# FC2 of a two-layer block as Strassen products over a finished FC1, with streamed weight sums

## The chip, the core and the metric

The kernel runs on one core of a Trainium2 chip. A core has a matrix engine (TensorE, PE in the profile), a vector engine (VectorE, DVE), a scalar engine (ScalarE, ACT), a general engine (GpSimd, POOL) and a sync engine (SP) that issues DMAs; 16 DMA engines move data between device memory and the on-chip memory SBUF. TensorE writes its sums to PSUM, which has eight banks of 512 float32 columns. The metric is the device time of one execution in microseconds, the median of several runs; lower is better.

## What is computed

Two layers, each an attention block and a feed-forward block (FFN) with a residual, over 2048 tokens of 640 channels:

```python
def _A_ref(x, wqkv, wo):                       # 32 heads of 20
    qkv = (x @ wqkv).reshape(B, S, 3, H, Dh).transpose(2, 0, 3, 1, 4)
    q, k, v = qkv[0], qkv[1], qkv[2]
    phi = lambda t: jnp.where(t > 0, t + 1, jnp.exp(t)) + 1e-6
    pq, pk = phi(q), phi(k)
    kv = jnp.einsum("bhsd,bhse->bhde", pk, v)
    z = jnp.einsum("bhsd->bhd", pk)
    num = jnp.einsum("bhqd,bhde->bhqe", pq, kv)
    den = jnp.einsum("bhqd,bhd->bhq", pq, z)[..., None] + 1e-6
    return (num / den).transpose(0, 2, 1, 3).reshape(B, S, D) @ wo

def _B_ref(x, w1, b1, w2, b2):                 # 640 -> 1728 -> 640
    r = jnp.maximum(jnp.einsum("bsd,df->bsf", x, w1) + b1, 0)
    return jnp.einsum("bsf,fd->bsd", r * r, w2) + b2

for _ in range(2):
    x = x + _A_ref(_layernorm(x, axis=-1), A_wqkv, A_wo)
    x = x + _B_ref(_layernorm(x, axis=-1), B_w1, B_b1, B_w2, B_b2)
```

## The kernel before

Every large product is made of three matmuls in the type float32r, as `mm3` does: each operand is split into a high half (a copy rounded to float32r, made by ScalarE) and a low half (the rest, a subtraction on VectorE), and high x low, low x high and high x high are added in PSUM. The tokens are 16 tiles of 128, or 4 groups (`NG`) of 4 tiles (`TG`).

A layer has three parts.

*The first stage* walks over the 16 tiles. Each is normed (`ln_stats`, `ln_apply`), turned so that the channels stand on the partitions, split, and multiplied with the q and k columns of wqkv (`part`). `Phi` applies the feature map. `g_part` and `gt_part` add the products of k features and x into G and GT, from which the small matrix M is made that stands for all of attention behind the q features. Turning a tile is VectorE's transpose of 32x32 blocks (`blocks_T`) followed by 16 copies on ScalarE that put the blocks in place (`blocks_move`); the first tiles of a layer are turned by TensorE (`transpose5`). The q part of the tiles in `LATE` is computed after the loop (`late_q`). In layer 0 this stage also prepares the FFN's weights (`Prep`): it loads a unit, splits it, and keeps it in device memory as `kept_w`. A unit is 128 rows of w2, or 128 columns of w1, with both halves, 640 KB. `PREP` says how many are done at each tile.

*The turn to the FFN* builds M and carries the first four tiles through the attention output, their residual, norm and turn.

*The FFN* runs group by group, and in a group chunk by chunk over the 1728 hidden channels (`NF` = 14 chunks, the last of 64). `fc1` computes a chunk for the 512 tokens of the group, 15 matmuls of 512 columns; `act` applies bias, relu and square and splits the result (one ScalarE and three VectorE operations of 128x512); `fc2` of the chunk before adds its part to the five outputs of the group (the 512 first columns of the four tiles, and the 128 last columns of all four as one turned "strip"), 5 x 3 matmuls of 512 columns. So FC1 and FC2 alternate every 3.4 us. At the end of a group the strip is turned back (`strip_turn`), and the sums are added to x1, which had been kept in device memory (`f_bias` stores it with the bias b2, `x1_load` loads it). The units of chunks 4 and 7 stay in SBUF (`RESIDENT`); the others come through a ring of six buffers (`load_ring`), 24 units a group.

Between the matmuls of a group stands the side work for the next one: the denominators of attention (`b_ops`), the turn and split of the q features, the attention output, residual, norm, turn and split of x. `single` does it tile by tile (group 1 of a layer), with 30 matmuls of 320 columns a tile; `side` with `Pair` does it for two tiles at once with seven Strassen products of 54 matmuls (groups 2 and 3), whose mixed operands are made by `m_turns` and `s_turns`. Where each step stands is written by hand: `events` maps a group, a chunk and a place to the steps. Each engine works strictly in the order in which its instructions are written, SP's queue of DMAs too, and waits at the head of its queue for whatever its next instruction needs. The last group of layer 0 prepares the first tiles of layer 1 in the same way (`side_last`).

## Time and profile before

| | |
|---|---|
| median of 3 runs | 1351.71 us (1351.32 to 1351.85) |
| span of the profiled execution | 1349.9 us |
| TensorE clock granted | 1.000 |
| layer 0: first stage and turn / four FFN groups | 0 to 255 us / 255 to 679 us |
| layer 1: first stage and turn / four FFN groups | 679 to 922 us / 922 to 1346 us |
| DMA traffic | 253.44 MB, mean 188 GB/s |

The page gives for each engine the time in which it executes something; matmuls overlap, so a row's mean duration (389 ns for 512 columns) is not the spacing at which they follow one another. Rows of groups read: line, engine, operation, out<-in, shape, count, busy us, mean ns of one, idle us before them and what ended it. Rows of the timeline read: start us, length us, engine, line, operation, out<-in, shape, count. Rows of the windows read: stretch, its length, then busy us and number of instructions of PE, PEld (weight loads), DVE, ACT and POOL, the granted clock, the busy share of the DMA engines and GB/s. A row of DMA issues gives KB each and the us from issue to landing.

### The profile page before, as it was taken

The numbers are of one execution on the slowest core, as the hardware profiler recorded it, in microseconds if no ns is written. First come the engines' busy times: TensorE is split into PE (matmuls) and PEld (weight loads), VectorE is DVE, ScalarE is ACT, GpSimd is POOL, SyncE is SP. The second block draws the span as 40 slices with busy tenths as digits, with TensorE's granted clock in tenths as the row PEclk, the third lists the DMA queues.
The fourth block names the chain that finished last, engine by engine and source line by source line (L and its number), as shares of the span: only waits on it lengthen the run. The fifth ranks groups of instructions, "written<-read, shape, count | busy, mean of one in ns | idle before, by whom it ended". The sixth has DMA issues, their size and how long they took to land.

```text
span 1349.9 us, 18967 instructions
## 1 busy us (share of the span) xinstructions
PE 1342.1 (99%) x6797; PEld 1158.3 (86%) x6797; DVE 911.7 (68%) x1627; ACT 770.3 (57%) x1932; POOL 123.4 (9%) x174
## 2 busy tenths in 40 slices
PE   9999999999999999999999999999999999999998
PEld 8888998888888888888888899988888888888887
DVE  7888757777777676643467676677778667775323
ACT  5878858676546448411447688494756446464110
POOL 2222210000000000000012232100000000000000
PEclk9999999999999999999999999999999999999999
DMA  6787835574665475387521115156546646644734
GB/s 205 254 301 269 284 86 177 192 275 145 212 237 174 158 292 170 117 327 293 184 98 51 48 40 155 41 206 255 173 157 232 216 150 223 233 167 140 287 125 158
DMA packets 85635, 253.44 MB, mean 188 GB/s; under 512 B 11030, under 2 KB 19606, under 8 KB 84902
## 3 DMA queue, kind: packets, MB, share of 16 engines
q1 hardware_dynamic: 85398, 252.04, 53.7%
q8 instruction: 54, 0.88, 0.3%
q14 instruction: 39, 0.32, 0.1%
q10 hardware_dynamic: 144, 0.20, 0.0%
HBM read 193.50 MB, written 56.03 MB: 185 GB/s over the span
## 4 chain that ended last, share of the span: by engine, by line
PE 92%; DVE 3%; ACT 3%; DMA 1%; issue 1%; POOL 0%; SPq 0%; DVEq 0%; ACTq 0%
PE PS L395 34%; PE PS L1064 28%; PE PS L1114 28%; ACT z L381 2%; PE PS L911 1%; PE PS L924 1%; DMA st<-in_A_wqkv_dram 1%; PE PS L726 0%; DVE bn L352 0%; DVE xr L658 0%; DVE e L498 0%; DVE xTb L131 0%; DMA Mr<-Mc 0%; DVE r L499 0%; PE PS L1128 0%
## 5 line engine op out<-in xcount | busy, mean ns | idle before, releaser
L381 ACT ACTIVATE z<-y 32x160 f32<-32x160 f32 x1424 | 475.8, 334 | 75.2 <-DVE y L372 59.0
L1064 PE MATMUL PS<-xTb,u 128*128 128x512 f32 x1400 | 333.8, 390 | 1.0 <-DVE xTb L131 1.0
L1064 PEld LDWEIGHTS PS<-xTb,u 128*128 128x128 f32 x1400 | 261.6, 188 | 55.0 <-DVE xTb L131 1.5
L395 PE MATMUL PS<-kq,xT 128*128 128x320 f32 (+2 forms) x1575 | 284.4, 334 | 0.4 <-DVE GT L529 0.4
L1114 PE MATMUL PS<-u,h 128*128 128x512 f32 x1120 | 276.8, 390 | 0.0
L395 PEld LDWEIGHTS PS<-kq,xT 128*128 128x128 f32 x1575 | 250.1, 188 | 28.2 <-DVE rl L499 1.0
L1114 PEld LDWEIGHTS PS<-u,h 128*128 128x128 f32 x1120 | 208.5, 188 | 40.8
L1076 ACT ACTIVATE hr<-PS,b1sb 128x512 f32<-128x512 f32 x104 | 71.4, 687 | 297.6 <-PE PS L1064 296.9
L1077 DVE TENSOR_TENSOR hr<-hr 128x512 f32<-128x512 f32 x104 | 71.8, 690 | 217.4 <-ACT hr L1076 216.9
L395 PE MATMUL PS<-kh,xh 128*128 128x512 f32 x480 | 124.6, 393 | 0.0
L491 ACT ACTIVATE e<-PS 128x320 f32<-128x320 f32 (+4 forms) x128 | 53.5, 435 | 101.9 <-PE PS L395 93.5
L356 POOL TENSOR_SCALAR rs<-mv 128x1 f32<-128x1 f32 x64 | 28.0, 438 | 869.6 <-DVE mv L354 869.6
L395 PE MATMUL PS<-uM,pT 128*128 128x320 f32 x648 | 102.6, 309 | 0.7 <-DVE uM L940 0.7
L395 PEld LDWEIGHTS PS<-kh,xh 128*128 128x128 f32 x480 | 87.2, 188 | 15.6 <-DVE kh L690 0.4
L395 PEld LDWEIGHTS PS<-uM,pT 128*128 128x128 f32 x648 | 97.7, 188 | 3.1 <-DVE uM L940 1.2
L498 DVE TENSOR_SCALAR e<-e 128x320 f32<-128x320 f32 (+4 forms) x128 | 41.7, 325 | 80.0 <-ACT e L491 79.7
L1114 PE MATMUL PS<-h,u 128*128 128x512 f32 x280 | 79.0, 390 | 0.0
L1079 DVE TENSOR_TENSOR h<-hr,h 128x512 fp32r<-128x512 f32 x104 | 72.0, 693 | 3.6
L687 POOL TENSOR_TENSOR acc<-acc,r 128x640 f32<-128x640 f32 x30 | 53.8, 1795 | 198.5 <-DVE r L499 198.5
L1114 PEld LDWEIGHTS PS<-h,u 128*128 128x128 f32 x280 | 52.2, 188 | 10.8 <-DVE h L1090 0.4
L1064 PE MATMUL PS<-xTb,uw 128*128 128x512 f32 x240 | 57.0, 389 | 0.0
L499 DVE SCALAR_TENSOR_TENSOR r<-PS,e 128x512 f32<-128x512 f32 (+2 forms) x104 | 51.1, 492 | 5.8 <-ACT e L491 2.4
(126 smaller groups left out, 1353.9 us busy)
## 6 DMA issues: line engine op xcount, KB each, us to landing
u<-kept_w SPq DMA_DIRECT2D x184, 640.0 KB, 4.3
x<-x SPq DMA_DIRECT2D x48, 320.0 KB, 6.3
kept_w<-uprep SPq DMA_DIRECT2D x23, 640.0 KB, 4.9
pqt<-pq SPq DMA_DIRECT2D x32, 320.0 KB, 5.6
x<-xr SPq DMA_DIRECT2D x32, 320.0 KB, 2.4
st<-in_B_w_dram SPq DMA_DIRECT2D x22, 320.0 KB, 5.6
pq<-r SPq DMA_DIRECT2D x20, 320.0 KB
kept_kq<-kq SPq DMA_DIRECT2D x10, 640.0 KB, 5.7
```

Source lines behind the costliest of these rows:

```text
L356: nc.gpsimd.tensor_scalar(rs, mv[:, 1:2], LN_EPS, None, op0=ALU.add)
L381: nc.scalar.activation(zv[j * B32 : (j + 1) * B32, :, i, :], yv[i * B32 : (i + 1) * B32, :, j, :], AF.Copy)
L395: nc.tensor.matmul(ps, a, b, start=first and i == 0, stop=last and i == 2)
L491: nc.scalar.activation(self.e[:, a:b], ps, AF.Exp)
L498: nc.vector.tensor_scalar(e, e, 1.0, PHI_EPS, op0=ALU.min, op1=ALU.add)
L499: nc.vector.scalar_tensor_tensor(out=self.r[:, a:b], in0=ps, scalar=0.0, in1=e, op0=ALU.max, op1=ALU.add)
L687: nc.gpsimd.tensor_tensor(out=acc, in0=acc, in1=r, op=ALU.add)
L1064: nc.tensor.matmul(ps, a[:, d, :], bb[:, d, :], start=d == 0 and i == 0, stop=d == DC - 1 and i == len(seq) - 1,)
L1076: nc.scalar.activation(r, ps, AF.Relu, bias=b1sb[:, c : c + 1])
L1077: nc.vector.tensor_tensor(out=r, in0=r, in1=r, op=ALU.mult)
L1079: nc.vector.tensor_tensor(out=h[:, 1], in0=r, in1=h[:, 0].bitcast(F32), op=ALU.subtract)
L1114: nc.tensor.matmul(ps, l, r, start=first and k == 0, stop=last and k == len(a) - 1)
```

## The change

FC2 becomes Winograd's form of Strassen's product: the 512 tokens of a group are two halves of 256, the hidden channels two halves of 7 x 128 (padded with zeros from 1728 to 1792), the 640 outputs two halves of 320. Seven products replace eight. For that, the group's FC1 is finished first and its squared result R stays in SBUF in float32. Then FC2 runs in 28 steps: the products in `ORDER`, each in four units of two row blocks (the last of one).

- `act` no longer splits; it writes R. `s_op` forms the four sums of quarters of R in place (VectorE), `u_hi` (ScalarE) and `u_lo` (VectorE) split the operand of a step into one of five slots (`arena`), four steps ahead.
- `fc2_step` is, for each row block and each of the two token tiles, three matmuls of 320 columns. The products of one output are chained in one PSUM bank (`CHAIN`), and `fc2_add` adds the state of the chain to x1 after a product, straight in SBUF; x1 is no longer stored and loaded again. There are no strips.
- The four sums of w2's quarters are formed in layer 0's first stage: `Prep` takes w1 units ("a") and pairs of w2 rows ("t"), for which GpSimd makes four sums (`mix`); one step of it stands at four places of each tile (`prep_step`). In the FFN one unit in four of each product stays in SBUF, the other three and all of w1 come through the ring.
- The attention output of all tiles is done singly; `side`, `Pair`, `m_turns` and `s_turns` are gone.
- x is turned in another order of channels (channel 5p + c in place of 128c + p; the rows of wqkv and w1 are loaded to match). In layer 1's first stage and in the FFN a tile is stored by GpSimd's DMA queue and loaded by four DMAs with 32 rows in runs of 160 elements (`spread_out`, `spread_in`); VectorE's transpose (`turn`) then finishes it, with no copies on ScalarE. In layer 0's first stage and the first two tiles of each FFN the 16 copies stay (`turn_move`).
- The bias b2 is added by GpSimd (`f_bias`). The pool of general tiles has 8 buffers in place of 12, and a new pool of 4 holds x1 and raw weights. The kq blocks are kept at tiles 11 to 15 instead of 6 to 15.

```diff
-RESIDENT = (4, 7)
 RING = 6
+KH = 7
+PAIRS = 4
+ORDER = (1, 5, 6, 2, 7, 3, 4)
+N_STEPS = len(ORDER) * PAIRS
+SLOTS = 5
+HT = GT // 2
...
-PREP = {t: 2 if t > 5 else 3 for t in range(2, 12)}
+PREP = {2: "aaa", 3: "t", 4: "t", 5: "aaaa", 6: "t", 7: "t", 8: "aaaa", 9: "t", 10: "t", 11: "aaa", 12: "t"}
+PREP_AT = range(1, 14)
...
-F_BUFS = 12
+F_BUFS, X_BUFS = 8, 4
+OUTS = (4, 7, 10, 13)
...
+        def mix(self):
...
+            def sub(out, x, y, op=ALU.subtract):
+                nc.gpsimd.tensor_tensor(out=out, in0=x, in1=y, op=op)
+
+            sub(q[:, lo], a[:, hi], a[:, lo])
+            sub(q[:, hi], b[:, hi], a[:, hi])
+            sub(a[:, hi], q[:, hi], a[:, lo], ALU.add)
+            self.raws.append(((p, (2, 3)), b, 2 * D))
+            self.raws.append(((p, (5, 7)), q, 2 * D))
+            self.raws.append(((p, (1, 6)), a, 2 * D))
...
+    def spread_out(src):
...
+        nc.gpsimd.dma_start(d, src)
+        return d
+
+    def spread_in(d):
+        z = ftile("z")
+        for j in range(JQ):
+            nc.sync.dma_start(
+                z[j * B32 : (j + 1) * B32].rearrange("p (i f) -> p i f", f=Q),
+                d[:, j * Q : (j + 1) * Q].rearrange("(i q) f -> q i f", q=B32),
+            )
+        return z
+
+    def turn(z):
+
+        y = ftile("y")
+        nc.vector.transpose(
+            out=y.rearrange("p (c i q) -> p i c q", c=DC, q=B32),
+            in_=z.rearrange("p (i q c) -> p i c q", c=DC, q=B32),
+        )
+        return y
...
+        def prep_step(t, i):
+            if layer == 0 and t in PREP_AT:
+                if i == 0:
+                    prep.mix()
+                prep.low()
+                prep.high()
+                if i == 3:
+                    prep.load(PREP.get(t + 1, ""))
...
         def f_bias(t):
 
-            v = xr.pop(t)
-            nc.vector.tensor_tensor(out=v, in0=v, in1=b2bc, op=ALU.add)
-            nc.sync.dma_start(x1d[t], v)
+            v = xr[t]
+            nc.gpsimd.tensor_tensor(out=v, in0=v, in1=b2bc, op=ALU.add)
...
+        def comb(out, x, y, k, op):
+            nc.vector.tensor_tensor(out=quad(*out, k), in0=quad(*x, k), in1=quad(*y, k), op=op)
...
+        def u_hi(g, n):
+            v, u = unit(g, n)
+            nc.scalar.activation(u[:, 0], v, AF.Copy)
+
+        def u_lo(g, n):
+            v, u = unit(g, n)
+            nc.vector.tensor_tensor(out=u[:, 1], in0=v, in1=u[:, 0].bitcast(F32), op=ALU.subtract)
...
+        def fc2_step(g, n, i, first, last):
...
+            for p in range(b - a):
+                h, l = (u[:, j, p, i * P : (i + 1) * P] for j in range(2))
+                for e, (x, y) in enumerate(((h, w[:, 1, p]), (l, w[:, 0, p]), (h, w[:, 0, p]))):
+                    nc.tensor.matmul(
+                        ps, x, y, start=opens and k == 0 and p == 0 and e == 0,
+                        stop=k == PAIRS - 1 and p == b - a - 1 and e == 2, skip_group_check=True,
+                    )
...
+        def single(g, i):
...
+            n = NF + (1, 5, 9, 13)[i]
+            at(g, n, load)
+            steps(lambda: x_split(t), (g, n + 4), (g, n + 5), (g, n + 6))
+
+        def ffn_events(g):
...
+            for n in range(PAIRS + 1, N_STEPS):
+                at(g, s + n - 4, lambda n=n: u_hi(g, n))
+                at(g, s + n - 4, lambda n=n: u_lo(g, n))
...
+            at(g, 2, lambda: load_kq(0))
+            for c, n in ((1, 5), (2, 13), (3, 21), (4, 25)):
+                at(g, s + n, lambda c=c: load_kq(c))
...
         for g in range(NG):
             for c in range(NF):
                 ps = fc1(g, c)
                 wu.load_ring()
+                act(c, ps)
+                run(g, ("pe", c))
+                run(g, c)
...
+            for n in range(last if tail else N_STEPS):
+                for i in range(2):
+                    fc2_step(g, n, i, False, False)
+                wu.used(g, ORDER[n // PAIRS], n % PAIRS)
+                wu.load_ring()
+                run(g, NF + n)
```

829 lines of the change are left out of this document (315 added, 514 removed).

## The prediction

> **What bounds the kernel now.** I read the page first, then the PE rows by form, then the timeline for the spacing of matmuls.
>
> ```profile
> span 1349.9 us, 18967 instructions
> PE 1342.1 (99%) x6797; PEld 1158.3 (86%) x6797; DVE 911.7 (68%) x1627; ACT 770.3 (57%) x1932; POOL 123.4 (9%) x174
> ...
> PEclk9999999999999999999999999999999999999999
> ...
> PE 92%; DVE 3%; ACT 3%; DMA 1%; issue 1%; POOL 0%; SPq 0%; DVEq 0%; ACTq 0%
> ```
>
> TensorE is busy in 1342.1 of 1349.9 us at an undisturbed clock, and 92% of the chain that ended last is matmuls. Only 7.8 us are left between them. So the time can fall only if TensorE gets less work, and it rises as soon as another engine makes it wait. The forecast is a count of matmuls, plus the waits that the new side work may cause.
>
> A busy PE is not yet a price, since matmuls overlap. The price is the distance between starts:
>
> ```profile
> 240.06 4.56 PE L395 MATMUL PS<-uM,pT 128*128 128x320 f32 x30
> 244.46 4.57 PE L395 MATMUL PS<-kq,xT 128*128 128x320 f32 x30
> ...
> 265.44 3.56 PE L1064 MATMUL PS<-xTb,u 128*128 128x512 f32 x15
> 268.84 2.88 PE L1114 MATMUL PS<-u,h 128*128 128x512 f32 x12
> ...
> 1342.02 0.60 PE L1128 MATMUL PS<-ident,strip 128*128 128x128 f32 x4
> 1342.38 3.69 PE L1114 MATMUL PS<-u,h 128*128 128x512 f32 x15
> ```
>
> 30 matmuls of 320 columns take 244.46 - 240.06 = 4.40 us, so 146.7 ns each; 15 of 512 columns take 3.40 us, so 226.7 ns each. That is 0.417 ns a column and a fixed 13.4 ns. The four strip transposes take 0.36 us.
>
> **The change on TensorE.** The counts, by form (FC2 is L1114, the attention output is what reads pT or uS):
>
> ```profile
> L1114 PE MATMUL PS<-u,h 128*128 128x512 f32 x1120 | 276.8, 390 | 0.0
> L1114 PE MATMUL PS<-h,u 128*128 128x512 f32 x280 | 79.0, 390 | 0.0
> L1114 PE MATMUL PS<-uw,h 128*128 128x512 f32 x192 | 46.1, 389 | 0.0
> L1114 PE MATMUL PS<-h,uw 128*128 128x512 f32 x48 | 13.5, 389 | 0.0
> ...
> L395 PE MATMUL PS<-uM,pT 128*128 128x320 f32 x648 | 102.6, 309 | 0.7 <-DVE uM L940 0.7
> L395 PE MATMUL PS<-uT,uS 128*128 128x320 f32 x144 | 25.0, 309 | 0.0
> L395 PE MATMUL PS<-uM,uS 128*128 128x320 f32 x72 | 11.8, 308 | 0.0
> L395 PE MATMUL PS<-uT,pT 128*128 128x320 f32 x48 | 8.3, 309 | 0.0
> ```
>
> FC2 before: 1640 matmuls in 8 groups, 205 each (13 chunks of 3 passes and one of 2, by 5 outputs), so 205 x 226.7 = 46.5 us a group. After: 7 products x 7 row blocks x 2 token tiles x 3 passes = 294 of 320 columns, so 294 x 146.7 = 43.1 us. The gain is 3.34 us a group, **26.7 us** in all: a tenth fewer columns, of which the 89 extra fixed costs take a quarter back. The 32 strip transposes go: 8 x 0.36 = **2.9 us**. The attention output was 912 matmuls and becomes 32 tiles x 2 halves x 5 x 3 = 960: 48 x 146.7 = **7.0 us** lost. FC1 and the first stage keep their matmuls. Net: -26.7 - 2.9 + 7.0 = **-22.6 us**.
>
> On the Trainium skill's page "TensorE: Matmul & The Clock Gate", section "Back-to-back issue gap", a sustained stream of weight load and matmul is given as about 81 ns at 128 columns and 131 ns at 512. By a line through these (an estimate) 320 columns would cost 106 ns, and FC2 would go from 205 x 131 = 26.9 to 294 x 106 = 31.2 us a group, 35 us lost in all. The rows above differ from both figures, so the measurement decides.
>
> **The side work in the FFN.** FC2 now stands in one block of 28 steps (1.76 us a step, 0.88 every fourth), and what VectorE does there was spread over FC1 before. Its spacings:
>
> ```profile
> 486.55 0.69 DVE L1079 TENSOR_TENSOR h<-hr,h 128x512 fp32r<-128x512 f32 x1
> 487.16 0.55 DVE L1284 TENSOR_TENSOR pT<-z,pT 128x384 fp32r<-128x384 f32 x1
> 487.74 2.01 DVE L1267 TENSOR_TENSOR z<-z 128x256 f32<-128x256 f32 x5
> ...
> 498.36 0.49 DVE L1335 TENSOR_TENSOR su<-PS,uu 128x320 f32<-128x320 f32 x1 [0.66 <-PE PS L395]
> 498.76 0.48 DVE L1335 TENSOR_TENSOR xr<-PS,xr 128x320 f32<-128x320 f32 x1
> 499.16 0.88 DVE L352 BATCH_NORM_STATS2 bn<-xr 128x6 f32<-128x320 f32 x2
> ...
> 505.34 0.85 DVE L372 STREAM_TRANSPOSE y<-xn 128x640 f32<-128x640 f32 x1
> 506.11 0.78 DVE L1335 TENSOR_TENSOR xr<-su,xr 128x640 f32<-128x640 f32 x1
> ```
>
> From start to start 512 columns cost 0.61 us, 256 cost 0.40, a PSUM addition of 320 costs 0.40, a transpose 0.77. One FC2 block holds 23 low halves (17 x 0.61 + 6 x 0.40 = 12.8), 13 sums of R (9 x 0.61 + 4 x 0.40 = 7.1), 12 additions (4.8), four turns and low halves of x (4 x 1.5 = 6.0), the last tile's addition and norm (0.8 + 0.9 + about 0.8) and the next tile's denominator and scaling (about 3.5 from the same widths): 36.7 us of 43.1. The low half of a unit is asked for 4 steps (6.2 us) before TensorE needs it, so VectorE may lag by some 4.9 us (6.2 less the high half on ScalarE, about 0.65, and the low half itself) before a matmul waits. It fits, with little to spare. The bias addition moves to POOL, and that is not free:
>
> ```profile
> 118.63 1.62 POOL L687 TENSOR_TENSOR acc<-acc,r 128x640 f32<-128x640 f32 x1 [7.09 <-DVE r L499]
> 119.33 1.61 DVE L131 TENSOR_TENSOR xh<-xt,xh 128x640 fp32r<-128x640 f32 x1
> 129.66 0.82 DVE L131 TENSOR_TENSOR xh<-xt,xh 128x640 fp32r<-128x640 f32 x1
> ```
>
> Beside a POOL operation of 1.62 us the same VectorE subtraction takes 1.61 instead of 0.82 us. One such bias falls into FC2: 0.8 us more, 37.5 in all (87%). I book **+2 us** for the six groups that carry side work. The lower bound is 0 (the lag absorbs all); the upper is the slower rival below. ScalarE loses the 16 block moves of each x tile (5.5 us, the row at 130.43 below), and its high halves fit.
>
> The weights: without the pairing, FC2 streams 3 of 4 units of each product. Including the next FC1's six, that is 18.5 full units of 640 KB, and ten transfers of 320 KB: 15.4 MB in 43.1 us, 357 GB/s. The rows:
>
> ```profile
> u<-kept_w SPq DMA_DIRECT2D x184, 640.0 KB, 4.3
> ...
> x<-xr SPq DMA_DIRECT2D x32, 320.0 KB, 2.4
> ...
> kq<-kept_kq SPq DMA_DIRECT2D x5, 1280.0 KB, 7.2
> ...
> 142.00:155.00 13.00, 13.00 (x80) 12.13 (x79) 11.63 (x24) 11.63 (x31) 4.66 (x5) 1.00 0.79 304
> 155.00:168.00 13.00, 13.00 (x78) 11.91 (x77) 9.27 (x19) 11.94 (x32) 3.33 (x3) 1.00 1.01 334
> ```
>
> 334 GB/s filled the engines once (share 1.01), with many short runs in it; 304 took 0.79, which makes about 385 when full. If four of FC1's six units come late, 297 GB/s do, and FC1 needs only 13 units in its 62 us (47 of its own, 13 of attention output). So I book nothing for starved weights; from below, nothing can be gained, and the price if the cover goes is a rival. At the end of layer 0 the last kq block is asked for when its slot comes free after step 24: 4.4 us of steps and the first 12 of 15 matmuls of the next stage (2.7 us) stand over its 7.2 us, so 0 to 1 us once, inside the 2.
>
> **The first stage of layer 0.** The weight sums of FC2 are made here. Before, 24 units were split in it; after, 14 of w1 and 28 pieces of w2, 38.5 full widths, so 14.5 more on ScalarE and VectorE, over tiles 1 to 13, and 28 POOL sums of 320 columns.
>
> ```profile
> 126.56 1.35 ACT L244 ACTIVATE uprep<-st 128x640 fp32r<-128x640 f32 x2
> 127.82 0.41 ACT L491 ACTIVATE e<-PS 128x320 f32<-128x320 f32 x1
> ...
> 127.43 1.55 DVE L248 TENSOR_TENSOR uprep<-st,uprep 128x640 fp32r<-128x640 f32 x2
> 128.90 0.32 DVE L498 TENSOR_SCALAR e<-e 128x320 f32<-128x320 f32 x1
> ...
> 130.43 5.51 ACT L381 ACTIVATE z<-y 32x160 f32<-32x160 f32 x16
> ```
>
> A piece costs 0.63 us on ScalarE and 0.73 on VectorE: 9.1 and 10.7 us more. A POOL sum takes about 0.8 (half of 1.62) and, by the pair of rows above, may hold VectorE 0.4: up to 11 us. From 142 to 168 us ScalarE is already busy 11.6 and 11.9 of each 13 us, and tile 9 and tiles 11 to 13, whose queries are left for later, have less TensorE time (30 x 146.7 + 15 x 226.7 ns = 7.8 us, and the few into GT) than 5.5 us of moves and five splits take. There it must overflow. ScalarE's excess over tiles 9 to 13 is some 4 us, and little slack catches it: I book **+4 us**, between 0 (it only lags) and 20 (both engines' additions end up in line). Layer 1's turn through memory is begun a whole tile (15 x 3 x 226.7 ns = 10.2 us and more) before it is used, and two transfers of the lengths below 4.3 us fit: nothing.
>
> **What costs nothing.** x1 no longer goes to memory and back: 64 transfers of 320 KB fewer, hidden before and gone now. VectorE and TensorE read x with a stride of five elements in the transposes that stay; no row shows a strided one. From below nothing, from above double time: 20 + 15 transposes on TensorE, some 3 us, and on VectorE 0.8 us a tile, which has room outside the overfull tiles; I take nothing, since matmul and transpose rows follow the element count. The f ring shrinks from 12 to 8 buffers, but the x rows and the raw weights leave it for their own four. The store of a bounced tile waits on POOL's queue for VectorE's norm, ahead of acc and rs; its load waits on SP's queue for that store, ahead of the next x load, which is three tiles early (over 20 us).
>
> **The sum.** 1349.9 - 22.6 + 2 + 4 = 1333.3 us of span. The median of the runs is 1.8 us above the span, so **1335 us**. Start and end stay (one addition and half a row's store behind the last matmul, as now).
>
> **Rivals.** *The turned x comes late* (slower). At four steps of each FC2 block VectorE waits for a tile that went to memory and back in 640-byte runs, asked for four steps (6.2 us) earlier, behind weight loads in SP's queue. The low halves stand behind the waiting transpose. Rows speak of 2.4 to 4.3 us, 320 KB and 640 KB; against them, the queue is far fuller here. With the 4.9 us of lag it bites from about 11 us of landing; at 13 us, 2 us are lost at 24 turns: +48 - 22.6, **1377 us**. The break-even is 0.94 us a turn. The Trainium skill, "DMA: Bandwidth & Descriptors", section "Rules for kernel authors", warns against turning data by a plain DMA with a rearranged pattern and speaks of a factor of 19; 19 x 2.4 would be 46 us of landing (an estimate), which no run here shows, and here the runs stay whole.
>
> *The first stage overflows in earnest*: 16 instead of 4 us, **1347**. For it, the two full windows; against, ScalarE still pauses and the work is spread in four pieces a tile.
>
> *Weights starve*: at 334 GB/s the 15.4 MB take 46.1 us, 3.0 more in each of 8 groups, 24 us against 22.6: **1353**. Against it, the six slots of lead.
>
> *It doesn't do what it says*: if narrow matmuls waited for their weight loads, at the 188 ns that one load lasts, FC2 would take 294 x 188 = 55.3 us, 70 us more in all: **1428**.
>
> ```profile
> L395 PEld LDWEIGHTS PS<-uM,pT 128*128 128x128 f32 x648 | 97.7, 188 | 3.1 <-DVE uM L940 1.2
> ```
>
> But these very loads pass at 146.7 ns a pair: loads overlap.
>
> **How the numbers follow.** Forecast 0.60 (1327 to 1344); overflow 0.14; late turns 0.18; starved weights 0.06; paced loads 0.02. The range starts at 1327, 2 us under the case without any stall (1329), and goes to 1356, over the overflow and the starved case and the mild turns (1 us each); beyond lie about 0.2. Within 0.2% (2.7 us) a measurement can't tell this kernel from no change. Faster: forecast, most of overflow and some of starved, 0.73; same 0.07; slower 0.20.
>
> **What would show it.** FC2's rows should number 2352 of 128x320, 146.7 ns apart; a wider spacing refutes the count. PE's idle time should stay under 14 us, most of the new part before 180 us. If VectorE's transposes of x in FC2 wait for a DMA and matmuls of FC2 for its low halves, the late turns are it; if matmuls wait for u, the weights. The forecast is wrong if TensorE's busy time has not fallen by about 22 us, or if its idle time grows by over 15.

## The result and the profile after

| | median | runs | profiled span | granted clock |
|---|---|---|---|---|
| before | 1351.67 us | 1351.32 to 1351.85 | 1349.9 us | 1.000 |
| after | 1427.86 us | 1426.03 to 1432.52 | 1427.7 us | 0.978 |

The ratio is 1.0568 (95% interval 1.0549 to 1.0588): 76 us slower, where 17 us faster was forecast. First the page of the changed kernel: its span, the engines' busy time, and the chain that ended last.

```profile
span 1427.7 us, 20898 instructions
...
PE 1352.0 (95%) x7525; PEld 1221.1 (86%) x7525; DVE 992.1 (69%) x1679; ACT 662.1 (46%) x1490; POOL 232.2 (16%) x277
...
PE 53%; DVE 25%; ACT 12%; DMA 4%; issue 4%; POOL 2%; SPq 1%; DVEq 0%; POOLq 0%; ACTq 0%
```

TensorE had 92% of the chain before and has 53% now; VectorE went from 3% to 25%, ScalarE from 3% to 12%. No engine is fuller than TensorE. The chain hops between engines that wait for each other. To see where, I cut the timeline of TensorE at the first matmul that reads G, the first of FC1 and the first of the next layer; layer 1's FFN ends with its last matmul (us):

| stage | before | forecast | after | above the forecast |
|---|---|---|---|---|
| layer 0: first stage | 201.5 | 205.5 | 228.9 | 23.4 |
| layer 0: turn to the FFN | 53.6 | 53.6 | 58.0 | 4.4 |
| layer 0: FFN | 423.8 | 413.5 | 446.6 | 33.1 |
| layer 1: first stage | 189.8 | 189.8 | 193.8 | 4.0 |
| layer 1: turn to the FFN | 53.6 | 53.6 | 57.9 | 4.3 |
| layer 1: FFN | 423.8 | 413.5 | 439.0 | 25.5 |

(The forecast column is the sum of the prediction laid on the stages: 22.6 us less and 2 more on the two FFNs, 4 more on layer 0's first stage.) So the forecast was missed in the FFN by 59 us, and in layer 0's first stage by 23.

The matmuls themselves did as counted. The rows of FC2 by form, and two starts in the timeline:

```profile
L1212 PE MATMUL PS<-u,arena 128*128 128x320 f32 x1680 | 266.1, 316 | 14.2 <-DVE arena L1196 14.2
...
L1212 PE MATMUL PS<-uw,arena 128*128 128x320 f32 x672 | 109.5, 310 | 4.9 <-DVE x L1225 4.9
```

```profile
383.06 4.56 PE L1212 MATMUL PS<-u,arena 128*128 128x320 f32 x30
387.46 1.92 PE L1212 MATMUL PS<-uw,arena 128*128 128x320 f32 x12
```

2352 matmuls, and 30 of them in 4.40 us, 146.7 ns each. Now the first two groups of layer 0's FFN in windows, each group as FC1 with the attention outputs, then FC2 (columns: PE, PEld, DVE, ACT, POOL busy, granted clock, DMA share, GB/s). By the count the first kind takes 205 matmuls of 226.7 ns (46.5 us) and four outputs of 4.4 us, 64.1 us, and the second 43.1 us.

```profile
286.90:362.80 75.90, 68.96 (x325) 59.44 (x326) 42.54 (x69) 35.41 (x87) 8.16 (x12) 0.93 0.59 213
362.80:412.20 49.40, 46.07 (x296) 45.68 (x295) 44.43 (x74) 15.24 (x29) 3.98 (x5) 0.93 0.78 253
412.20:483.60 71.40, 67.37 (x327) 58.65 (x326) 40.92 (x63) 35.18 (x86) 9.02 (x12) 0.95 0.56 207
483.60:529.50 45.90, 43.83 (x297) 43.17 (x296) 41.68 (x71) 15.32 (x29) 3.02 (x4) 1.00 0.85 277
```

More is lost in FC1 (12 and 7 us) than in FC2 (6 and 3), and in FC1 VectorE is busy for only 42.5 of 75.9 us and ScalarE for 35.4: both idle for about half of a stage in which TensorE waits for them. The timeline of all engines shows one such wait whole:

```profile
321.82 3.83 PE L460 MATMUL PS<-uM,pTs 128*128 128x320 f32 x25
...
324.23 0.78 POOL L389 DMA_DIRECT2D xb<-xn  x1 [0.97 <-DVE den L698]
324.42 2.90 DVE L701 TENSOR_TENSOR pqt<-pqt,den 128x640 f32<-128x640 f32 x1
325.03 1.59 POOL L736 TENSOR_TENSOR x<-x,b2bc 128x640 f32<-128x640 f32 x1
...
325.49 10.39 PE L1143 MATMUL PS<-xTb,u 128*128 128x512 f32 x45
327.35 0.84 DVE L417 STREAM_TRANSPOSE y<-pqt 128x640 f32<-128x640 f32 x1
328.23 2.77 ACT L426 ACTIVATE z<-y 32x160 f32<-32x160 f32 x8 [10.23 <-DVE y L417]
...
331.02 0.69 ACT L1155 ACTIVATE R<-PS,b1sb 128x512 f32<-128x512 f32 x1
331.74 2.75 ACT L426 ACTIVATE z<-y 32x160 f32<-32x160 f32 x8
331.75 0.69 DVE L1156 TENSOR_TENSOR R<-R 128x512 f32<-128x512 f32 x1 [3.55 <-ACT R L1155]
...
335.18 0.69 DVE L1196 TENSOR_TENSOR arena<-R,arena 128x512 fp32r<-128x512 f32 x1 [2.74 <-ACT arena L1192]
...
339.91 0.88 DVE L1313 TENSOR_TENSOR x<-PS,x 128x320 f32<-128x320 f32 x2
...
340.55 7.07 PE L460 MATMUL PS<-uM,pTs 128*128 128x320 f32 x30 [4.67 <-DVE x L1313]
```

The attention output of one tile ends at 325.5 us; its addition on VectorE (L1313) comes at 339.9, and the next tile's output needs the same two banks. In between each queue waits for the other's head: ScalarE stands 10.23 us for the transposed y (L417), with the relu of a chunk behind it; VectorE stands 3.55 us for that relu, which came only after eight block moves (2.77 us), then 2.74 us for the operand's high half, which stands behind eight more. The y was late itself: its scaling (L701), 0.82 us elsewhere, took 2.90 beside GpSimd's bias (L736); the store of the bounced tile (L389) also stands beside it, but holds nothing, as a_bias_dve shows below. At last TensorE runs the 30 matmuls in 7.07 us in place of 4.56.

### The profile page after: what moved, and what is told of

Same layout as the page of the kernel before. It is cut to its first block, busy times and chain, and to the rows that moved or that the text cites. A ratio compares the mean times of both kernels' runs of the same rounds, so it can differ in the third digit from the quotient of the medians.

```text
span 1427.7 us, 20898 instructions
## 1 busy us (share of the span) xinstructions
PE 1352.0 (95%) x7525; PEld 1221.1 (86%) x7525; DVE 992.1 (69%) x1679; ACT 662.1 (46%) x1490; POOL 232.2 (16%) x277
## 4 chain that ended last, share of the span: by engine, by line
PE 53%; DVE 25%; ACT 12%; DMA 4%; issue 4%; POOL 2%; SPq 1%; DVEq 0%; POOLq 0%; ACTq 0%
PE PS L460 22%; PE PS L1212 16%; PE PS L1143 13%; ACT z L426 7%; DVE R L1173 2%; DVE arena L1196 2%; DVE bn L358 2%; DVE pqt L701 2%; DVE R L1156 2%; DMA z<-xb 2%; ACT R L1155 2%; DMA kept<-uprep 1%; DVE x L1313 1%; POOL rs L363 1%; DVE xn L368 1%
## 5 line engine op out<-in xcount | busy, mean ns | idle before, releaser
L1212 PE MATMUL PS<-u,arena 128*128 128x320 f32 x1680 | 266.1, 316 | 14.2 <-DVE arena L1196 14.2
L1212 PEld LDWEIGHTS PS<-u,arena 128*128 128x128 f32 x1680 | 257.3, 194 | 16.0 <-DVE arena L1196 15.8
L426 ACT ACTIVATE z<-y 32x160 f32<-32x160 f32 x512 | 171.3, 335 | 163.4 <-DVE y L417 157.4
L1196 DVE TENSOR_TENSOR arena<-R,arena 128x512 fp32r<-128x512 f32 x224 | 140.0, 634 | 72.0 <-ACT arena L1192 71.3
L1192 ACT ACTIVATE arena<-R 128x512 fp32r<-128x512 f32 x224 | 122.5, 571 | 142.3 <-PE PS L1212 102.7
L460 PE MATMUL PS<-uM,pTs 128*128 128x320 f32 x720 | 117.1, 323 | 19.8 <-DVE x L1313 19.7
L460 PEld LDWEIGHTS PS<-uM,pTs 128*128 128x128 f32 x720 | 113.2, 199 | 25.7 <-ACT R L1155 13.5
L1212 PE MATMUL PS<-uw,arena 128*128 128x320 f32 x672 | 109.5, 310 | 4.9 <-DVE x L1225 4.9
L1212 PEld LDWEIGHTS PS<-uw,arena 128*128 128x128 f32 x672 | 101.0, 188 | 6.8 <-DVE x L1225 6.5
L446 ACT ACTIVATE z<-y 32x160 f32<-32x160 f32 x272 | 90.8, 334 | 5.6 <-DVE y L432 2.5
L1173 DVE TENSOR_TENSOR R<-R 128x512 f32<-128x512 f32 (+1 forms) x128 | 87.7, 696 | 0.0
```

Source lines behind the costliest of these rows:

```text
L426: nc.scalar.activation(zv[j * B32 : (j + 1) * B32, :, i, :], yv[i * B32 : (i + 1) * B32, :, j, :], AF.Copy)
L446: nc.scalar.activation(zv[j * B32 : (j + 1) * B32, :, i, :], yv[i * B32 : (i + 1) * B32, j], AF.Copy)
L460: nc.tensor.matmul(ps, a, b, start=first and i == 0, stop=last and i == 2)
L1173: nc.vector.tensor_tensor(out=quad(*out, k), in0=quad(*x, k), in1=quad(*y, k), op=op)
L1192: nc.scalar.activation(u[:, 0], v, AF.Copy)
L1196: nc.vector.tensor_tensor(out=u[:, 1], in0=v, in1=u[:, 0].bitcast(F32), op=ALU.subtract)
```

## The experiments on the FFN

All runs by stage (us); each is told below. Stages and spans are those of one profiled execution, and f, g, j, k, l, m and n were executed only that once. How far a stage moves by itself can be read in the table: the six kernels with the first stage of the changed one (after, a, b, e, h, i) have 228.4 to 230.1 there, and the seven with its FFN (after, c, d, f, g, j, l) have 441.3 to 450.4 and 434.6 to 441.7. Differences inside these ranges say little.

| run | first stage, layer 0 | turn | FFN 0 | FFN 1 | span |
|---|---|---|---|---|---|
| before | 201.5 | 53.6 | 423.8 | 423.8 | 1349.9 |
| after | 228.9 | 58.0 | 446.6 | 439.0 | 1427.7 |
| a_bias_dve | 229.7 | 55.0 | 437.1 | 431.0 | 1404.8 |
| b_moves_later | 228.4 | 58.0 | 443.9 | 436.3 | 1420.8 |
| c_no_sums | 222.7 | 58.0 | 447.2 | 434.6 | 1417.8 |
| d_store_often | 247.4 | 58.0 | 450.4 | 437.2 | 1446.4 |
| e_no_side | 229.6 | 58.0 | 416.6 | 411.7 | 1369.9 |
| f_zero_stores | 202.4 | 58.0 | 449.3 | 436.0 | 1399.1 |
| g_row_stores | 222.2 | 57.9 | 444.9 | 439.8 | 1418.8 |
| h_ffn_order | 230.1 | 54.9 | 442.0 | 442.5 | 1421.6 |
| i_ffn_ahead | 228.6 | 55.0 | 417.0 | 412.9 | 1366.2 |
| j_dma_turn | 247.1 | 58.0 | 441.3 | 437.0 | 1439.4 |
| k_plain_order | 224.0 | 57.4 | 444.6 | 433.5 | 1412.5 |
| l_sums_dve | 234.9 | 58.0 | 448.8 | 441.7 | 1438.8 |
| m_store_lag | 223.9 | 54.9 | 416.6 | 412.9 | 1359.3 |
| n_w1_late | 217.1 | 54.9 | 418.9 | 412.9 | 1355.2 |
| o_both | 215.4 | 54.9 | 417.1 | 413.0 | 1351.6 |
| p_prep_early | 211.6 | 54.9 | 422.0 | 412.9 | 1353.6 |
| q_prep_early2 | 212.6 | 54.9 | 417.5 | 412.9 | 1349.3 |
| r_six_late | 211.4 | 54.9 | 421.3 | 412.9 | 1350.9 |

**a_bias_dve: the bias back on VectorE.**

```diff
-            nc.gpsimd.tensor_tensor(out=v, in0=v, in1=b2bc, op=ALU.add)
+            nc.vector.tensor_tensor(out=v, in0=v, in1=b2bc, op=ALU.add)
```

> The bias b2 is added by VectorE instead of GpSimd (32 additions of 128x640). Theory 'shared access': beside GpSimd's DMA write and bias a VectorE operation with two SBUF inputs takes 2.6 to 2.9 us instead of 0.8, and these delays are what makes the matmuls wait in the FFN and at its start. Then each turn from attention to the FFN falls from 58.0 to about 54 us, the 11.4 us in which matmuls wait for the x addition and the 6.4 us for the operand slots in layer 0's FFN fall by more than half, and the kernel gets about 20 us faster (1408). Rival 'order': the instruction order of ScalarE and VectorE is what binds in the FFN; then only the two turns gain (8 us, 1420), and VectorE's 0.74 us more per tile eats part of it.

1407.96 us, 1.0418 times before (1.0388 to 1.0448); the span is 22.9 us shorter, although VectorE now does the 32 additions itself (26.0 us). Its busy time still fell, from 992.1 to 979.5 us: on GpSimd each bias held VectorE for (992.1 - 979.5 + 26.0) / 32 = 1.2 us, where the prediction gave one 0.8. And it had counted only the one in each FC2; the other three of a group and the four in a row at the start of an FFN were taken as hidden, and they were not: 3.0 us of each turn came back.

The time is the one that the first theory named, but not all of its signs came. In layer 0's FFN TensorE's waits for the operand slots fell from 6.4 to 1.2 us, those for the attention output's addition only from 11.4 to 7.3, and those for the additions of the products (L1225) rose from 3.0 to 6.8. A second cause is left. And the run tells which operation of GpSimd it was. This is the place in the timeline shown above, with the store still on GpSimd:

```profile
321.27 0.78 POOL L389 DMA_DIRECT2D xb<-xn  x1 [0.97 <-DVE den L698]
321.46 0.82 DVE L701 TENSOR_TENSOR pqt<-pqt,den 128x640 f32<-128x640 f32 x1
```

Beside the store alone the scaling takes its 0.82 us.

**b_moves_later: the block moves and the split one chunk later.**

```diff
-            on(b - 5, lambda: blocks_move(yzp[t], (0, 1)))
-            on(b - 4, lambda: blocks_move(yzp[t], (2, 3)))
+            on(b - 4, lambda: blocks_move(yzp[t], (0, 1)))
+            on(b - 3, lambda: blocks_move(yzp[t], (2, 3)))
```

> Only the order in the FFN is changed: the 16 block moves of the attention features come one chunk later after their transpose (chunks b-4 and b-3 instead of b-5 and b-4), the split of the result at b-2 instead of b-3. Theory 'order': ScalarE stands at the moves, waiting up to 10 us for the transpose, with the next chunk's relu behind them, and VectorE then waits for the relu; apart by a chunk, both waits go, the additions of x come in time, and the 11.4 us (layer 0) and about 7 us (layer 1) of matmuls waiting for x mostly vanish, with the slow clock after them: 20 to 25 us faster (1405). Rival 'shared access': the waits for x stay within a third, the kernel stays at 1420 to 1428.

1425.24 us, 1.0546 (1.0498 to 1.0594). The waits for L1313 are gone and others are in their place: 10.3 us in layer 0 and 12.0 us in layer 1 for the split operand of the same output (pTs). The queues form a ring of waits: each stands at its head for something that stands behind the head of another. Shifting one part of the ring moves the wait.

**e_no_side: only the FFN's own work on VectorE and ScalarE.** In `single`, the denominators, transposes, moves, splits, norm, bias and turns of tiles 5 to 15 are left out, and every output reads one old operand. The outputs' additions and the statistics of the norm stay.

> The attention work of tiles 5 to 15 inside the FFN blocks is left out on VectorE, ScalarE and the queues (denominators, transposes, moves, splits, LayerNorm apply, biases, turns); TensorE keeps every matmul, with one old operand, and the sums from PSUM stay. Side theory: the Strassen blocks on their own run at TensorE's pace, so that each FFN stage takes 412 to 417 us where it took 446.6 and 439.0, span about 1370. Rival, the products themselves (their banks, their sums, the streamed weights) do not keep up: the FFN stages stay above 430 us, span above 1400.

1371.17 us, 1.0144 (1.0100 to 1.0187). FC2 takes what was counted, the second group in windows:

```profile
396.60:460.80 64.20, 64.20 (x328) 56.12 (x327) 21.22 (x41) 12.03 (x19) 3.31 (x6) 1.00 0.55 194
460.80:503.90 43.10, 43.10 (x296) 43.10 (x295) 27.50 (x53) 13.27 (x23) 1.15 (x2) 1.00 0.75 244
```

So the products, their banks and the streamed weights keep up, and the side work makes the whole loss of the FFN. It may be too much work, or work in the wrong order; the next two runs separate these.

**h_ffn_order: four edits and other places.**

```diff
-OUTS = (4, 7, 10, 13)
+OUTS = (5, 8, 11, 13)
...
-            on(b + 1, add)
+            on(b, add)
...
-        nc.gpsimd.dma_start(d, src)
+        nc.sync.dma_start(d, src)
```

(with the bias on VectorE, and two of the sums of R at chunks 11 and 13.)

> Bias on VectorE, the sum of the attention output one chunk earlier, its places at chunks 5, 8, 11, 13 instead of 4, 7, 10, 13, two weight-of-R sums pulled into FC1, bounced stores issued by SyncE instead of GpSimd. Order theory (VectorE has the time, but in the wrong places): the FFN stages go from 437.1 and 431.0 (bias on VectorE alone) to 415 to 422 each, time about 1380 us. Rival, VectorE is simply too full beside the products: they stay above 428 each, time above 1395.

1422.89 us, 1.0526 (1.0481 to 1.0572): a miss, worse than the bias alone. Its second group, first TensorE, then VectorE:

```profile
457.16 5.85 PE L1143 MATMUL PS<-xTb,u 128*128 128x512 f32 x25
466.30 6.17 PE L460 MATMUL PS<-uM,pTs 128*128 128x320 f32 x30 [3.29 <-DVE x L1313]
```

```profile
462.05 0.42 DVE L1196 TENSOR_TENSOR arena<-R,arena 128x256 fp32r<-128x256 f32 x1 [2.50 <-ACT arena L1192]
...
465.67 0.88 DVE L1313 TENSOR_TENSOR x<-PS,x 128x320 f32<-128x320 f32 x2
```

The output that ended at 457.2 is added at 465.7 even though its addition was now asked for earlier: VectorE stood before it, waiting for ScalarE's high halves, which stood behind block moves. And chunks 11 and 13 leave only two chunks between two outputs. By itself this run looks like support for "too full".

**i_ffn_ahead: places 4, 7, 10, 13 again, and each result asked for one place later than it is made.**

```diff
-            on(b - 8, lambda: b_load_pq(t))
-            on(b - 6, lambda: b_den(t))
-            on(b - 5, lambda: b_blocks(t))
+            on(b - 9, lambda: b_load_pq(t))
+            on(b - 7, lambda: b_den(t))
+            on(b - 6, lambda: b_blocks(t))
...
-            on(b + 2, lambda: f_bias(t))
+            at(g + 1, 3 * i + 2, lambda: f_bias(t))
...
-            steps(lambda: x_split(t), (g, n + 4), (g, n + 5), (g, n + 6))
+            steps(lambda: x_split(t), (g, n + 5), (g, n + 6), (g, n + 7))
...
-                at(g, s + n - 4, lambda n=n: u_hi(g, n))
+                at(g, s + n - 5, lambda n=n: u_hi(g, n))
```

(`u_lo` of the first units one chunk after its `u_hi`; `ffn_events` entered ahead of `single`, so that operands and sums come first in a place; and the four edits above.)

> The FFN side work set anew, places 4, 7, 10, 13 kept: bias on VectorE and only in the next group's FC1; sum of the attention output in the chunk of its matmuls; denominators and transposes one chunk earlier than their moves; the first half of an operand of FC2 one place ahead of the second; operands and sums ahead of the attention work within a place; turns one step later; bounced stores from SyncE. Theory, head of line (ScalarE and VectorE have the time, but wait for one another in their queues): the FFN stages fall from 446.6 and 439.0 us to 414 to 424 each, the turns to 55.0, the time to about 1380 us. Rival, VectorE too full beside the products: they stay above 430.

1366.35 us, 1.0106 (1.0077 to 1.0136). The same two groups in windows:

```profile
283.60:349.10 65.50, 64.50 (x325) 56.04 (x326) 43.59 (x78) 35.53 (x87) 2.38 (x6) 1.00 0.69 251
349.10:392.40 43.30, 43.30 (x297) 43.30 (x296) 38.09 (x68) 16.12 (x28) 0.79 (x2) 1.00 0.92 288
392.20:456.40 64.20, 64.20 (x328) 56.12 (x327) 41.62 (x73) 35.96 (x87) 2.37 (x6) 1.00 0.65 228
456.40:499.60 43.20, 43.20 (x296) 43.20 (x296) 37.27 (x66) 17.33 (x31) 0.79 (x2) 1.00 0.93 296
```

FC2 takes 43.2 us with VectorE at 37.3 to 38.1 of it, and FC1 with its outputs 64.2. VectorE's busy time in the whole kernel is 979.4 us, against 979.5 with the bias alone: the same work, 38.6 us less time. "Too full" is out, and the order of the queues is shown as the cause of what was left after the bias. (The bounced stores went to SyncE's queue as well; h_ffn_order has that too, and gained nothing by it.) How an output is added now, TensorE first, then VectorE:

```profile
409.25 4.56 PE L460 MATMUL PS<-uM,pTs 128*128 128x320 f32 x30
413.64 10.39 PE L1143 MATMUL PS<-xTb,u 128*128 128x512 f32 x45
423.87 4.56 PE L460 MATMUL PS<-uM,pTs 128*128 128x320 f32 x30
```

```profile
411.64 0.49 DVE L1313 TENSOR_TENSOR x<-PS,x 128x320 f32<-128x320 f32 x1 [0.17 <-PE PS L460]
413.84 0.49 DVE L1313 TENSOR_TENSOR x<-PS,x 128x320 f32<-128x320 f32 x1 [1.71 <-PE PS L460]
```

VectorE waits for TensorE, not the other way round, and has the banks free 9.5 us before they are needed. Which of the edits carries how much was not tried one by one; only that the four of h_ffn_order with their places do not do it.

## The experiments on layer 0's first stage

Three theories: VectorE's or ScalarE's time, the memory (transfers, SyncE's queue), GpSimd's sums. Windows of the changed kernel:

```profile
60.00:100.00 40.00, 36.50 (x183) 30.48 (x182) 35.36 (x59) 31.84 (x76) 16.07 (x17) 1.00 0.82 278
100.00:140.00 40.00, 36.88 (x190) 31.97 (x189) 34.68 (x58) 30.76 (x77) 16.02 (x16) 0.96 0.77 262
140.00:180.00 40.00, 35.00 (x176) 30.51 (x175) 35.65 (x56) 29.84 (x74) 15.75 (x16) 0.91 0.81 268
```

**c_no_sums** leaves GpSimd's 28 sums of w2 out and splits the plain rows; **l_sums_dve** gives them to VectorE (`nc.gpsimd` to `nc.vector` in `mix`).

> The four GpSimd sums of w2's quarters in layer 0's first stage are left out: the raw quarters are split and stored in their place, with the same loads, copies, subtractions and stores; the buffer of one sum is not allocated either. Theory 'shared access' for the first stage: the stage (0 to 228.9 us, 27.4 longer than before) gives back 15 us or more. Rival 'stores': ScalarE's waits for a free buffer whose store has not landed (14.5 us) and the later loads stay, and the stage gives back under 6 us.

> The 28 sums of FC2's weights go from GpSimd to VectorE (28 of some 0.45 us, 12.6 us in all). Shared-access theory (what GpSimd's sums cost VectorE is more than their own time there): the first stage falls from 228.9 by 3 to 8 us. Rival, VectorE's own time: it grows by 3 to 10.

Without the sums the stage is 6.2 us shorter, which is near the rival's end of the first expectation; with them on VectorE it is 6.0 us longer, as the rival of the second had it. Their price is some 6 us; the other 21 come from elsewhere, and GpSimd is the better place for them.

**f_zero_stores** keeps all loads and stores and does no splitting and no sums; **g_row_stores** splits everything and stores one row of 128.

> Splitting and mixing of the FFN weights in the first stage is left out; every store to memory takes the same zeroed tile, so that loads, stores and their issues stay. Engine theory: the first stage, 228.9 us in the changed kernel and 201.5 before, falls to 201 to 207. Memory theory (transfers and the queue of SyncE are the limit): it stays at 222 or more. Both in part: in between.

> The other half: splitting and mixing stay, but a store writes one row of 128 (only the first FC1 unit is stored whole, and every FFN load reads it, with the same bytes per load). Engine theory: the first stage stays at 222 or more. Memory theory: it falls to 201 to 207. If both this one and the one with zeroed stores fall most of the way, it is the coupling: a buffer is held until its store has landed.

202.4 us without splits, 222.2 without most of the stored bytes. The windows of f_zero_stores:

```profile
100.00:140.00 40.00, 40.00 (x207) 34.73 (x206) 29.45 (x51) 28.41 (x73) 9.31 (x9) 1.00 0.97 330
140.00:180.00 40.00, 40.00 (x240) 37.20 (x239) 30.83 (x54) 34.72 (x89) 12.73 (x12) 1.00 1.00 354
```

The DMA engines are full (share 0.97 and 1.00) and TensorE does not notice: 40.00 of 40. The work of ScalarE, VectorE and GpSimd sets the stage; which of the three, this run does not say. But cutting the stored bytes gave 6.7 us, so part of that work also waits for stores.

**d_store_often** stores after each of the four splits of a tile; **m_store_lag** stores a second time per tile, ahead of the place's own split, on top of i_ffn_ahead.

```diff
                 prep.low()
+                prep.store()
                 prep.high()
```

```diff
+                if i == 2:
+                    prep.store()
                 prep.low()
                 prep.high()
```

> In layer 0's first stage finished weight units are stored at each of the four places of a tile instead of together at the start of the next tile. Theory 'stores': ScalarE stops waiting for the six split buffers (14.5 us, longest 6.0), VectorE follows, and the stage falls from 228.9 to about 215 us. Rival 'shared access': the waits for buffers go and the stage still loses under 5 us, because VectorE is full anyway (34 to 38 of each 40 us). A third way: the queue of SP now stands at each store for VectorE, the loads of x and weights come later, and the stage gets longer.

> On top of the re-ordered FFN work (first stage 228.6 us there): stores of finished FFN weight units are issued twice per tile, the second time before the place's own split, so that they wait for a split of the place before at most. Buffer theory (ScalarE waits for a buffer whose store came late): the first stage falls to 222 or less. VectorE theory: within 3 us of 228.6. Queue theory (SyncE stands at a store and loads come late, as with a store after every split): 233 or more.

Storing at once makes it 247.4: SyncE's queue stands at these stores for VectorE's low halves for 104 us in all (10.9 in the changed kernel), and the loads behind them come late. One place later it is 223.9, between the expectations. ScalarE's wait for a buffer whose store has not landed shows in the row of the high halves, i_ffn_ahead first, then m_store_lag:

```profile
L290 ACT ACTIVATE uprep<-st 128x640 fp32r<-128x640 f32 x13 | 9.6, 737 | 14.9 <-DMA kept<-uprep 14.5 <-issue 0.3
```

```profile
L290 ACT ACTIVATE uprep<-st 128x640 fp32r<-128x640 f32 x13 | 9.6, 735 | 4.6 <-DMA kept<-uprep 4.5
```

10 us of that wait are worth 4.7 us of the stage.

**j_dma_turn** turns x in layer 0 through memory from tile 4 on and so takes 64 us of moves from ScalarE.

> Layer 0 turns x from tile 4 on through memory, as layer 1 does, so that ScalarE loses twelve times 16 moves of 0.334 us (64 us) in the first stage, and VectorE nothing. If ScalarE sets that stage: 228.9 us falls to 218 or less. If VectorE does: it stays within 4 us of 228.9. If the added traffic on SyncE's queue weighs: 233 or more.

247.1 us, as the third case had it. Whether ScalarE bounds the stage, the run cannot tell, since the added traffic outweighs what was taken off it. The loads of the bounced tiles join SyncE's queue, and ScalarE, relieved of its moves, waits 34.2 us for turned tiles (L123 behind VectorE's y) and 21.3 us for loads (L290).

**n_w1_late** splits four of w1's 14 units in the first group's FC1, on top of i_ffn_ahead.

```diff
-            self.w1 = list(range(NF))
+            self.w1 = [c for c in range(NF) if c not in W1_LATE]
...
+        if layer == 0:
+            for c in W1_LATE:
+                at(0, 0, lambda c=c: w1_load(c))
+                at(0, c - 3, lambda c=c: w1_late(c))
+                at(0, c - 1, lambda c=c: w1_store(c))
```

> On top of the re-ordered FFN work: four of FC1's units (6 to 9) are split in the first group's FC1 instead of the first stage, from raw rows staged in the part of R that is not written yet. 3.3 us of VectorE and 2.9 of ScalarE leave the first stage, four loads and four stores too. VectorE theory: the first stage falls by 2 to 4 us from 228.6; buffer theory: by 5 or more. The first FFN stage, 417.0, stays within 3 us in both.

217.1, 11.5 us less for 3.3 us of VectorE: as the buffer theory had it, though the list of loads per tile became thinner with it, and ScalarE's work, four loads and four stores left the stage too. The FFN pays 1.9 us.

**k_plain_order** reads and writes in order in all transposes of the changed kernel.

> The interleaved order of features is taken out of all the transposes (on VectorE and TensorE they read and write rows in order), so the features meet the wrong rows of the weights; nothing else changes. Price of the strides: 1.37 against 0.845 us on 57 transposes is 30 us of VectorE. If VectorE's fullness sets the first stage and FC2, some 15 to 25 us of them show: first stage 220 to 224, FFN stages 3 to 6 us shorter each. If these transposes lie beside other work: under 5 us in all.

The span is 15.2 us shorter: 4.9 in the first stage, which is clear, and 7.5 in the FFNs, where 444.6 lies inside the range of the kernels with an untouched FFN and 433.5 only 1.1 us below it. The rows of the changed kernel, then one from before:

```profile
L407 DVE STREAM_TRANSPOSE y<-z 128x640 f32<-128x640 f32 x40 | 54.8, 1371 | 8.3 <-DMA z<-xb 7.9 <-issue 0.4
...
L432 DVE STREAM_TRANSPOSE y<-xt 128x640 f32<-128x640 f32 x13 | 17.9, 1376 | 0.7
```

```profile
L372 DVE STREAM_TRANSPOSE y<-xt 128x640 f32<-128x640 f32 x29 | 24.5, 845 | 0.9
```

57 strided transposes (with the four of L432 on xn) cost 0.53 us more each, 30 us of VectorE. Of these 4.9 us show for certain in the time, and at most half.

## Can it be repaired?

**o_both** joins n_w1_late and m_store_lag; **p_prep_early** and **q_prep_early2** load the rows earlier (q_prep_early2 spares the short tile 9; its list against o_both's stands below), and **r_six_late** moves six units into FC1.

```diff
-PREP = {2: "aa", 3: "t", 4: "t", 5: "aaa", 6: "t", 7: "t", 8: "aaa", 9: "t", 10: "t", 11: "aa", 12: "t"}
+PREP = {2: "aaaa", 3: "t", 4: "t", 5: "aaaa", 6: "t", 7: "t", 8: "t", 9: "aa", 10: "t", 11: "t"}
```

> Both edits together on top of the re-ordered FFN work. If their gains add up as the buffer theory has it, the first stage comes to 217 us or less and the time to some 1355 us; as the VectorE theory has it, to 225 and 1363.

> The kernel with both first-stage edits, and the list of which FFN rows are loaded at which tile packed so that the last sums are made at tile 11 and not 12, with the same rows in all. If the crowding of VectorE beside the short tiles is what is left: the first stage falls from 215.4 to 209 to 212 us and the time to 1347 to 1351. If VectorE is full everywhere: it stays within 1 us, with the waits moved to earlier tiles.

> The same with tile 9, which is short, given two plain units in place of three sums' four, and four loads at once at the start. Expected as for the other list; if the early tiles cannot take it (their window of 20 to 60 us has VectorE at 36.6 of 40), waits appear before 60 us and it is longer by 1 to 3 us than the other list.

> As the kernel whose short tile 9 was lightened, with six FC1 units instead of four split in the first group's FC1 (units 6 to 11, two through one more staging buffer) and no rows of w1 loaded for tile 9. Two units are 1.6 us of VectorE's splits. If the splits are still what is left: the first stage goes from 212.6 to 207 to 210 us, the first FFN stage stays within 2 us of 417.5, and the time comes to 1346 to 1349 us. If it is the rest (sums, strides): the first stage stays above 211 and the time within 2 us of 1351.

| run | median | ratio to before (95%) |
|---|---|---|
| o_both | 1356.23 us | 1.0032 (1.0021 to 1.0043) |
| p_prep_early | 1353.89 us | 1.0014 (1.0005 to 1.0023) |
| q_prep_early2 | 1351.37 us | 1.0000 (0.9991 to 1.0010) |
| r_six_late | 1352.66 us | 1.0008 (0.9999 to 1.0017) |

The loss is gone, but no version passes the kernel before. o_both's stage, 215.4, is near what the buffer theory had (the two gains would add up to 212.4). p_prep_early's falls to 211.6 as expected, but its first FFN takes 422.0 instead of 417.1, and the time stays above the 1347 to 1351 expected. In q_prep_early2 ScalarE's wait for buffers is down to 0.7 us, and the stage still takes 212.6:

```profile
60.00:100.00 40.00, 39.30 (x203) 33.47 (x202) 38.23 (x65) 34.59 (x84) 16.92 (x17) 1.00 0.86 295
100.00:140.00 40.00, 38.01 (x193) 31.91 (x192) 39.04 (x66) 32.54 (x81) 17.25 (x17) 1.00 0.83 281
140.00:180.00 40.00, 37.25 (x200) 33.05 (x201) 37.05 (x59) 34.34 (x85) 19.48 (x20) 0.96 0.82 289
```

Now VectorE is nearly full (37.05 to 39.04 of 40), which it was not in the changed kernel (34.68 to 35.65). Two more units out of the stage (r_six_late) gave 1.2 us there, less than such a stage moves by itself, and cost 3.8 us in the FFN: the case in which the splits are not what is left. So in q_prep_early2 the two FFNs win 17.2 us on before (6.3 and 10.9), the first stage loses 11.1, the turns 2.6 and layer 1's first stage 3.3. What of the 11.1 is sums and what strides, was not tried in this version.

## Why the prediction was wrong

**The count of matmuls was right.** 2352 at 146.7 ns; layer 1's FFN in i_ffn_ahead is 10.9 us shorter than before, for 11.3 counted. The prediction's own test by TensorE's busy time was a poor one: busy time went up by 9.9 us, since slowed matmuls count as busy. Its test by idle time was sound: idle went from 7.8 to 75.7 us.

**The step that failed is "The side work in the FFN"**, in the sentences that the low half of a unit is asked for 4 steps ahead, so that VectorE may lag by some 4.9 us, that it fits, and that 2 us are booked. In their place the two FFNs took 59 us more than forecast: 17.5 us came back with the bias on VectorE (a_bias_dve), and 38.2 more with the other order (i_ffn_ahead). The load was sized well for i_ffn_ahead: 37.5 of 43.1 us forecast, 37.3 to 38.1 of 43.2 measured. That is in part luck, since its FC2 holds two sums of R and the bias less, and four transposes that are 0.53 us longer each than forecast. But a load that fits says nothing of the order. The prediction added up VectorE's instructions in FC2 and followed no queue through FC1, where the larger part was lost: it did not list what stands behind `blocks_move` on ScalarE (relu and high halves) and who waits for those (VectorE's squares and low halves, and behind them the addition that frees the banks). The block was not too full: with the order changed and the bias on VectorE, the FFNs take 417.0 and 412.9 us against the 413.5 forecast.

**The price of a GpSimd operation** was too small, 0.8 us for 1.2 measured, and so was its number: all 32 biases count, not six.

**The first stage** was booked at 4 us between 0 and 20, and it was 27.4, beyond the end that was to hold "both engines' additions end up in line". That they did so in full is not shown. The bound lacked two things: a buffer of a unit is held until its store has landed, with stores issued once a tile (4.7 us by m_store_lag), and the strides (4.9 us by k_plain_order). With the sums (6.2 us) that makes 15.8, each measured by itself; the rest was not divided further, and f_zero_stores shows only that it goes when the splits go.

**Strides** stood under "costs nothing", with 0.8 us a tile as the upper end. They cost 0.53 us a tile, and 4.9 to 15.2 us of time by k_plain_order; the argument that rows follow the element count did not hold for a VectorE transpose.

**Streamed weights**: nothing was booked, and 3.7 us are seen in i_ffn_ahead, in the last group of layer 0 alone, where the kq blocks are loaded too. The last kq block costs 2.5 us (0 to 1 forecast).

**The rivals.** "The turned x comes late" is out as a cause: in the L407 row above VectorE waited 7.9 us for z in 40 turns, where the rival needed 48 us. The overflow was the right place with too small a price (16 us for 27.4). Starved weights and paced loads did not come. That the paced loads' 1428 us is the measured median is chance: by the two starts of FC2 shown first, its matmuls follow one another at 146.7 ns, not at 188. The slower side had been given 0.20, all of it to mechanisms other than the one that came: a ring of waits between two queues, neither of which is full.

## What to carry to other kernels

When side work is set anew beside a full TensorE, write down for one period what stands in each in-order queue, and follow every instruction that waits to those behind it and to who waits for these; busy shares cannot show a ring. Ask an engine for a result one place later than the neighbour can have it, and put what frees a bank ahead of what only prepares. If an experiment with half of the reordering gets worse, that does not refute the order: test with the work left out first, so that the floor is known.

## What the runs showed of the hardware

**A short idle of TensorE can cost twice.** Two waits of the same length, the changed kernel first, then i_ffn_ahead:

```profile
148.19 2.92 PE L460 MATMUL PS<-kh,xh 128*128 128x512 f32 x6 [2.89 <-DVE kh L756]
```

```profile
148.63 1.66 PE L460 MATMUL PS<-kh,xh 128*128 128x512 f32 x6 [2.88 <-DVE kh L756]
```

After 2.89 us of idle six matmuls took 2.92 us, after 2.88 us elsewhere 1.66; after 4.67 us thirty took 7.07 for 4.56, and the granted clock of the window was 0.93. Over layer 0's FFN TensorE idled 20.8 us in the changed kernel and 4.7 in i_ffn_ahead, and the same matmuls were busy for 425.7 us at a granted clock of 0.97 and for 412.2 at 1.00: of the 29.6 us between the two kernels, 13.5 are slower matmuls. The Trainium skill's page "TensorE: Matmul & The Clock Gate", section "HAM oscillation — how this bites in real kernels", warns of idle gaps above about 3.4 us, and says under "What's actually happening" that the window runs freely; that the same gap slows or does not slow agrees with this, but here 2.9 us were enough.

**A GpSimd addition can hold a VectorE operation until it ends.** The scaling of q (L701), with two operands from SBUF, took 0.82 us alone. Of the twelve that met a bias in the changed kernel, six took 2.72 to 2.90 us and ended 0.7 us after the bias, and six kept their 0.82. Transposes (L417), with one operand, kept their 0.84 us beside a bias. The Trainium skill's page "SBUF — State Buffer", section "Who interferes with whom", describes one port pair of the two engines with an exclusive lock, for which a VectorE instruction with two SBUF inputs contends with a GpSimd instruction that reads SBUF; the trace agrees. Moving the biases to VectorE brought L701's mean from 1.19 to 0.83 us, with the bounced stores still issued by GpSimd.
